# Moving the first two steps of an MoE layer one place earlier between the attention units of a fused kernel

## The chip, the core and the metric

The kernel runs on one core of one Trainium2 chip. The metric is the device time of one launch in microseconds (us), as the median of several executions on the chip. A core has five engines that run their own instruction streams in order and wait for each other by semaphores: TensorE (PE in the profile, with its weight loads as PEld), VectorE (DVE), ScalarE (ACT), GpSimd (POOL) and SyncE (SP), whose queue here issues every DMA.

## What is computed

A sliding-window attention with a few sink positions, whose output is the input of two dense two-matrix layers (called MoE in the code, though there is no routing):

```
scores = q @ k.T / 8                       # 2 batches, 8 heads, 768 positions, head size 64
keep   = key position < n_sink  or  0 <= distance < window      # 4 and 128
a      = softmax(where(keep, scores, -1e9));   x = a @ v        # x: 1536 tokens x 512
h = x @ w1_in;   x = (h * tanh(softplus(h))) @ w1_out           # 512 -> 2048 -> 512
h = x @ w2_in;   out = (h * clip(h + 3, 0, 6) / 6) @ w2_out
```

The weights come as 64-bit floats in HBM and are decoded on the core.

## The kernel before

**Tiling.** The 1536 tokens are twelve units of 128 positions of one batch. They are grouped into three blocks of four units, `BLOCKS = [[6, 7, 0, 1], [2, 3, 4, 5], [8, 9, 10, 11]]`; the MoE layers work on a block (512 tokens) at a time. All values that go into an MoE matmul are split into two fp16 halves, and each product is three matmuls (high by high, high by low, low by high).

**The first eight units** (blocks 0 and 1) are computed by the class `First` in fp32 and are emitted by `first_blocks` in the order 6, 7, 0, 1, 2, 3, 4, 5; its loop variable `n` counts them from 0, so n = 5, 6, 7 are units 3, 4 and 5. For each unit it emits `turn(0)` (transposes of the exponentials of heads 0 to 3, line 315, copied out of PSUM by ACT at 317 and DVE at 319; the sink columns at 323 to 326), the next unit's `scores(0)` (line 296; row minimum on DVE 300, exponential on ACT 304), the `outputs` of the unit before (line 356 transposes the result, 359 and 360 write it into the block's `xt`), `values(0)` (334 and 341), `turn(1)`, the next unit's `scores(1)`, `values(1)`, and `normalise` (347 to 350). The last unit, n = 7, has no next unit, so no scores lie between its parts.

**The last four units** (block 2) are emitted in small pieces by `gen_front` and `gen_back` in fp16, between the halves of later MoE steps, from the moment `open_late` has opened their buffers. Those buffers take the memory of the first units, so their first load (`load_unit`, 411) waits for the last `normalise`. Keys and queries of a late unit are loaded (411), split on ACT and DVE (431/432 for k, 439/440 for v, 457/458 for q), and transposed by a DMA (434 for `kt`, 460 for `qt`); the sinks go through `gen_sinks` (520 to 542, four small loads `vsn` among them). Then come the scores (480), minimum (487), exponential (494), the transposed probabilities `atg` (511) and the values (557 to 568).

**An MoE step** (`moe_steps`) takes two chunks of 128 of the 2048 inner columns for one block. `up` is 24 matmuls of 512 columns into two PSUM tiles (666 to 668), then the activation: for the first layer ACT 670 on each half, 678, 679, 680, DVE 683 twice, ACT 689 (high half of `g16`), DVE 690 (low half). `down` is 24 matmuls (725) that read that `g16`; it is emitted one step later (`LAG = 1`). Before a step, the weights it needs are decoded (208 to 210 and 216 on DVE, 213 on ACT), from two raw buffers that SP fills (166 and 170, 512 KB each). `hook`, called amid the steps, emits further pieces of weight decoding and, once the late buffers are open, of the late units.

**Order.** The generator `moe` is advanced by `next(moe)` inside `first_blocks` for its first two steps and run to its end after it. `up` of these steps reads block 0, which is complete with the `outputs` of n = 3, emitted at n = 4. What is written here is only the order of emission: the tile framework schedules the instructions and sets the order in which they stand on each engine.

Of the kernel before, what the change touches and what calls it, by code (L numbers as in the profile page):

```python
# [29 lines left out]
def attention_moe_moe2(  # L30
# [30 lines left out]
    w_a = main.enter_context(tc.tile_pool(name="w_a", bufs=KF // 2))  # L61
    st_p = main.enter_context(tc.tile_pool(name="st", bufs=STB))
    dec_p = main.enter_context(tc.tile_pool(name="dec", bufs=1))
    part_p = main.enter_context(tc.tile_pool(name="part", bufs=NPART))
    e_p = main.enter_context(tc.tile_pool(name="e", bufs=2))
    g_p = main.enter_context(tc.tile_pool(name="g", bufs=LAG + 1))
    ps_acc = main.enter_context(tc.tile_pool(name="ps_acc", bufs=4, space=PSUM))
# [95 lines left out]
    def fetch_w(layer, f):  # L163
        wi, wo = wsrc[layer]
        t = st_p.tile([128, 2, 512, 2], I32, tag="raw", name="raw")
        nc.sync.dma_start(
            out=t[:, 0].rearrange("p (k f) t -> p k (f t)", k=KD),
            in_=wi[:, f * 256:(f + 1) * 256].rearrange("(k p) f -> p k f", p=128),
        )
        nc.sync.dma_start(out=t[:, 1].rearrange("p f t -> p (f t)"), in_=wo[f * 128:(f + 1) * 128, :])  # L170
        return t

    def load_w():
        if nload[0] >= len(wseq):
            return
        layer, f = wseq[nload[0]]
        nload[0] += 1
        raw_t[layer, f] = fetch_w(layer, f)
# [9 lines left out]
    def gen_check():  # L188

        ahead = []  # L190
        for f in range(KF):
            ahead.append((f, fetch_w(0, f)))
            if len(ahead) > STB - 1:
                g, t = ahead.pop(0)
# [40 lines left out]
    def load_first(u, names="kqv"):  # L235
        b, i = divmod(u, NSB)
        rows = slice(i * 128, (i + 1) * 128)
        for nm, src, pool, tag in (("k", k, n_p, "n"), ("q", q, n_p, "n"), ("v", v, v_p, "v")):
            if nm in names:
                t = pool.tile([128, H, D], F32, tag=tag, name="first")  # L240
                nc.sync.dma_start(out=t, in_=src[b, :, rows, :].rearrange("h p d -> p h d"))
                qkv_n.setdefault(u, {})[nm] = t
# [121 lines left out]
    def first_blocks():  # L364
        us = [First(u) for u in first]
        for u in us[:2]:
            u.prep()
        us[0].scores(0)
        us[0].scores(1)
        for n, e in enumerate(us):  # L370
            f = us[n + 1] if n + 1 < len(us) else None
            if n + 4 < len(us):
                load_first(first[n + 4])
            e.turn(0)
            if f:
                f.scores(0)
            if f is None:
                next(moe)
            if n > 0:
                us[n - 1].outputs()  # L380
            e.values(0)
            if n + 2 < len(us):
                us[n + 2].prep()
            e.turn(1)
            if f:
                f.scores(1)
            if n == len(us) - 2:
                next(moe)
            e.values(1)
            e.normalise()  # L390
        us[-1].outputs()
# [303 lines left out]
    def down(st, span):  # L695
        layer, blk, f = st
        T = len(blocks[blk]) * 128
        per = per_bank(blk)
        g2 = gt.pop(st)
        fa, fb = span  # L700
        if f == fa:
            acc[layer, blk] = [ps_acc.tile([128, per * T if layer == 0 else DM], F32, tag="acc", name="acc") for _ in range(KD // per if layer == 0 else T // 128)]
        a = acc[layer, blk]

        parts = [(n, m) for n in range(len(a)) for m in range(per if layer == 0 else 1)]
        for i in range(2 * per):
            g16 = g2[:, :, i]
            w = wt[layer, 1, f + i]
            first, last = f + i == fa, f + i == fb - 1
            for c, (n, m) in enumerate(parts):  # L710
                if layer == 0:
                    wh = w[:, 0, c * 128:(c + 1) * 128]
                    wl = w[:, 1, c * 128:(c + 1) * 128]
                    mm = [(wh, g16[:, 0]), (wh, g16[:, 1]), (wl, g16[:, 0])]
                    o = a[n][:, m * T:(m + 1) * T]
                    end = m == per - 1
                else:
                    gh = g16[:, 0, c * 128:(c + 1) * 128]
                    gl = g16[:, 1, c * 128:(c + 1) * 128]
                    mm = [(gh, w[:, 0]), (gh, w[:, 1]), (gl, w[:, 0])]  # L720
                    o = a[n]
                    end = True
                for x, (l_, r_) in enumerate(mm):

                    nc.tensor.matmul(o, l_, r_, start=first and m == 0 and x == 0, stop=last and end and x == 2, skip_group_check=True)  # L725
                if last and end:
                    finish(layer, blk, n, a[n], span)
            if i % per == per - 1:
                hook()
# [39 lines left out]
    load_first(first[3])  # L769
    for _ in range(STB - 1):  # L770
        load_w()
# [24 lines left out]
    def moe_steps():  # L796
        pend = []
        fmax = 0
        for s, (cur, span) in enumerate(steps):
            layer, j, f = cur  # L800
            fend = layer * KF + f + 2 * per_bank(j)
            fmax = max(fmax, fend)
            stage = [x[:4] for x in STAGES].index((layer, j) + span)
            budget["lim"] = 2 * (fmax + AHEAD[stage])
            budget["chk"] = stage >= CHECK and not raw_t
            if f == span[0] and layer == 0 and j >= 2:
                att_side.until(("unit", blocks[j][-1]))
            budget["att"] = RATES[stage]
            dec_side.until(("dec", fend - 1))
            up(cur)  # L810
            yield
            pend.append((cur, span))
            while len(pend) > LAG:
                down(*pend.pop(0))
        for st in pend:
            down(*st)

    moe = moe_steps()
    first_blocks()
    p1.close()  # L820
    open_late()
# [179 lines left out]
STAGES = [(0, 0, 0, 4), (0, 1, 0, 10), (0, 0, 4, 16), (0, 1, 10, 16), (0, 2, 0, 16), (1, 0, 0, 8), (1, 1, 0, 8), (1, 0, 8, 16), (1, 1, 8, 16), (1, 2, 0, 16)]  # L1001
CHECK = 8
LAG = 1
STB = 2
P1N = 8
NWARM = 12
# [40 lines left out]
```

## Time and profile before

| | |
|---|---|
| Median of three runs | 624.52 us (624.19 to 625.42) |
| The profiled execution's own time | 623.05 us |
| Its span, first to last instruction | 621.3 us |
| PE busy in the span | 600.8 us, 97% |
| DVE, ACT, POOL busy | 376.0, 354.6, 14.2 us |
| Granted TensorE clock, mean | 0.998 of full speed |

The span lies 1.75 us below the execution's own time, and the profiled execution 1.47 us below the median of the runs. Times in the rows below count from the start of the span. Busy time is the time that an engine spends in instructions that the profile counts; ends of matmuls are modelled. The first eight attention units run until about 98.8 us, the first layer's steps on blocks 0 and 1 and the late units lie behind that, and the second layer fills the rest.

### The profile page before, as it was taken

How to read it: one execution, taken by the hardware profiler on the slowest of the kernel's cores; microseconds unless marked ns; L12 is line 12 of the kernel's file. 1: busy time of each engine (PE TensorE's matmuls, PEld its weight loads, DVE VectorE, ACT ScalarE, POOL GpSimd, SP SyncE). 2: the span in 40 equal slices, each digit the busy share in tenths (PEclk: the TensorE clock that was granted, in tenths of full speed). 3: DMA queues.
4: the chain of work that ended last, by engine and by line, in shares of the span. 5: the costliest groups of instructions: out<-in, count | busy, mean ns of one | idle time of the engine just before them, and what ended most of it. 6: DMA issues, size and time to landing. Idle time of an engine off the chain costs nothing.

```text
span 621.3 us, 8731 instructions
## 1 busy us (share of the span) xinstructions
PE 600.8 (97%) x3400; PEld 307.6 (50%) x3400; DVE 376.0 (61%) x688; ACT 354.6 (57%) x640; POOL 14.2 (2%) x28
## 2 busy tenths in 40 slices
PE   8999999899989999899999999999999999999995
PEld 5888865444444445444444444444444444444442
DVE  5678787889988554626988999844432322422221
ACT  5887676887788676647686765453343331413131
POOL 0010000600000000000000000000000000000000
PEclk9999999999999999999999999999999999999999
DMA  9865146897479313100344434598800100100002
GB/s 188 195 130 170 69 143 150 218 244 210 135 205 205 55 37 54 37 18 0 136 136 136 148 124 152 193 333 304 304 0 1 44 25 0 69 1 0 1 0 73
DMA packets 105832, 72.10 MB, mean 116 GB/s; under 512 B 73512, under 2 KB 98088, under 8 KB 105784
## 3 DMA queue, kind: packets, MB, share of 16 engines
q1 hardware_dynamic: 105784, 71.48, 41.3%
q8 instruction: 28, 0.46, 0.3%
q14 instruction: 20, 0.16, 0.1%
HBM read 60.43 MB, written 3.15 MB: 102 GB/s over the span
## 4 chain that ended last, share of the span: by engine, by line
PE 68%; DVE 14%; ACT 9%; DMA 4%; issue 3%; SPq 1%; ACTq 0%; DVEq 0%
PE acc L725 27%; PE h L666 9%; PE h L668 9%; PE h L667 9%; PE o L341 4%; PE s L296 3%; DVE g L690 2%; DVE e L683 2%; PE tp L315 2%; DVE p L209 2%; DVE p L210 2%; ACT w L213 1%; ACT e L678 1%; ACT e L679 1%; DVE w L216 1%
## 5 line engine op out<-in xcount | busy, mean ns | idle before, releaser
L666 PE MATMUL h<-xt,w 128*128 128x512 f16 x384 | 145.6, 379 | 1.3 <-DVE e L683 1.3
L667 PE MATMUL h<-xt,w 128*128 128x512 f16 x384 | 145.5, 379 | 0.0
L668 PE MATMUL h<-xt,w 128*128 128x512 f16 x384 | 145.5, 379 | 0.0
L725 PE MATMUL acc<-g,w 128*128 128x512 f16 x576 | 129.5, 379 | 2.7 <-DVE g L690 2.2
L725 PE MATMUL acc<-w,g 128*128 128x512 f16 x576 | 128.1, 379 | 0.0
L685 DVE SCALAR_TENSOR_TENSOR e<-e,h 128x512 f32<-128x512 f32 x48 | 32.8, 686 | 97.8 <-ACT e L672 97.8
L725 PEld LDWEIGHTS <-g 128*128 128x128 f16 x576 | 56.3, 98 | 68.0
L725 PEld LDWEIGHTS <-w 128*128 128x128 f16 x576 | 55.4, 98 | 69.0 <-issue 3.8
L672 ACT ACTIVATE e<-h,bias 128x512 f32<-128x512 f32 x48 | 32.7, 683 | 95.7 <-PE h L668 95.7
L690 DVE SCALAR_TENSOR_TENSOR g<-e,g 128x1024 f16<-128x1024 f32 x48 | 58.7, 1223 | 25.1 <-ACT g L689 24.9
L689 ACT ACTIVATE g<-e 128x1024 f16<-128x1024 f32 x48 | 50.6, 1055 | 31.7 <-DVE e L685 17.9
L668 PEld LDWEIGHTS <-w 128*128 128x128 f16 x384 | 37.6, 98 | 45.2
L667 PEld LDWEIGHTS <-w 128*128 128x128 f16 x384 | 37.6, 98 | 44.7 <-issue 1.3
L666 PEld LDWEIGHTS <-w 128*128 128x128 f16 x384 | 37.6, 98 | 44.6
L216 DVE SCALAR_TENSOR_TENSOR w<-p,w 128x1024 f16<-128x1024 f32 x32 | 39.1, 1222 | 14.5 <-ACT w L213 14.5
L213 ACT ACTIVATE w<-p 128x1024 f16<-128x1024 f32 x32 | 33.7, 1053 | 21.5 <-DVE p L210 21.1
L670 ACT ACTIVATE e<-h 128x512 f32<-128x512 f32 x48 | 28.3, 589 | 25.6 <-PE h L668 25.3
L186 ACT ACTIVATE y<-y 128x512 int32<-128x512 int32 x32 | 20.0, 625 | 37.0 <-DVE y L184 36.9
L683 DVE SCALAR_TENSOR_TENSOR e<-e,h 128x512 f32<-128x512 f32 x48 | 30.7, 681 | 16.9 <-ACT e L680 16.9
L209 DVE SCALAR_TENSOR_TENSOR p<-raw,p 128x1024 int32<-128x1024 int32 x32 | 39.1, 1223 | 0.7
L210 DVE SCALAR_TENSOR_TENSOR p<-raw,p 128x1024 int32<-128x1024 int32 x32 | 39.1, 1222 | 0.3
L304 ACT ACTIVATE d<-d,mins 128x272 f32<-128x272 f32 (+2 forms) x64 | 30.4, 479 | 6.6 <-DVE mins L300 6.6
(141 smaller groups left out, 582.6 us busy)
## 6 DMA issues: line engine op xcount, KB each, us to landing
raw<-in_moe_w_in_dram SPq DMA_DIRECT2D x48, 512.0 KB, 3.9
raw<-in_moe_w_out_dram SPq DMA_DIRECT2D x48, 512.0 KB, 5.1
first<-in_k_dram SPq DMA_DIRECT2D x8, 256.0 KB, 5.2
first<-in_q_dram SPq DMA_DIRECT2D x8, 256.0 KB, 5.0
first<-in_v_dram SPq DMA_DIRECT2D x8, 256.0 KB, 5.2
out_dram<-part SPq DMA_DIRECT2D x8, 256.0 KB, 2.2
nk<-in_k_dram SPq DMA_DIRECT2D x5, 256.0 KB, 3.2
nv<-in_v_dram SPq DMA_DIRECT2D x5, 256.0 KB, 4.2
```

What stands on the lines that cost most here:

```text
L209: nc.vector.scalar_tensor_tensor(out=p, in0=lo_w, scalar=29, in1=p, op0=ALU.logical_shift_right, op1=ALU.bitwise_or)
L210: nc.vector.scalar_tensor_tensor(out=p, in0=hi_w, scalar=-0x40000000, in1=p, op0=ALU.bitwise_and, op1=ALU.bitwise_or)
L213: nc.scalar.activation(out=w[:, :, 0, :], in_=pf, func=AF.Copy, scale=2.0 ** SW)
L216: nc.vector.scalar_tensor_tensor(out=w[:, :, 1, :], in0=pf, scalar=2.0 ** SW, in1=w[:, :, 0, :], op0=ALU.mult, op1=ALU.subtract)
L666: nc.tensor.matmul(o, wh, x[:, 0, c, :], start=c == 0, stop=False)
L667: nc.tensor.matmul(o, wh, x[:, 1, c, :], start=False, stop=False)
L668: nc.tensor.matmul(o, wl, x[:, 0, c, :], start=False, stop=c == KD - 1)
L683: nc.vector.scalar_tensor_tensor(out=e[:, i], in0=e[:, i], scalar=2.5, in1=hps[i], op0=ALU.subtract, op1=ALU.mult)
L685: nc.vector.scalar_tensor_tensor(out=e[:, i], in0=e[:, i], scalar=6.0, in1=hps[i], op0=ALU.min, op1=ALU.mult)
L689: nc.scalar.activation(out=gh, in_=e, func=AF.Copy, scale=sc)
L690: nc.vector.scalar_tensor_tensor(out=gl, in0=e, scalar=sc, in1=gh, op0=ALU.mult, op1=ALU.subtract)
L725: nc.tensor.matmul(o, l_, r_, start=first and m == 0 and x == 0, stop=last and end and x == 2, skip_group_check=True)
```

## The change

`first_blocks` advances `moe` for the units in the new constant `FILL = (5, 6)`, each time between `turn(1)` with the next unit's `scores(1)` and `values(1)`. The first step moves from n = 6 to n = 5 (unit 4 to unit 3). The second moves from n = 7 (unit 5), where it stood behind `turn(0)`, to n = 6 (unit 4). Nothing else is edited; the same instructions are in both programs. Lines behind the removed ones have numbers smaller by two in the changed kernel (668 for 670, 723 for 725).

```diff
             e.turn(0)
             if f:
                 f.scores(0)
-            if f is None:
-                next(moe)
             if n > 0:
                 us[n - 1].outputs()
...
             e.turn(1)
             if f:
                 f.scores(1)
-            if n == len(us) - 2:
+            if n in FILL:
                 next(moe)
             e.values(1)
             e.normalise()
...
+FILL = (5, 6)
```

The scheduled order changes on every engine from the first moved step to about 250 us; behind that it is the same but for buffer and semaphore choices. Three places matter to what follows.

On PE, the end of the first eight units, before (`d`, `ds` are exponentials, `tp` transposes in PSUM, `ats` sink columns, `xf` a unit's normalised result):

```order
L356 MATMUL tp<-ident,xf 128x128 x4
L334 MATMUL o<-vsb_331,ats 128x256
L341 MATMUL o<-first,at 128x64 x8
L315 MATMUL tp<-ident,d 128x128 x8
L325 MATMUL tp<-ident,ds 64x128
L334 MATMUL o<-vsb_331,ats 128x256
L341 MATMUL o<-first,at 128x64 x8
L356 MATMUL tp<-ident,xf 128x128 x4
```

and in the changed kernel, from the values of unit 4 on:

```order
L341 MATMUL o<-first,at 128x64 x8
L315 MATMUL tp<-ident,d 128x128
L325 MATMUL tp<-ident,ds 64x128
L356 MATMUL tp<-ident,xf 128x128 x4
L315 MATMUL tp<-ident,d 128x128 x4
L334 MATMUL o<-vsb_331,ats 128x256
L341 MATMUL o<-first,at 128x64 x8
L315 MATMUL tp<-ident,d 128x128 x4
L325 MATMUL tp<-ident,ds 64x128
L334 MATMUL o<-vsb_331,ats 128x256
L341 MATMUL o<-first,at 128x64 x8
L356 MATMUL tp<-ident,xf 128x128 x4
```

Before, the second step's 24 matmuls stood right ahead of the first row; now they stand ahead of the values of unit 4, and nothing but two short transposes parts those values from the transposes (356) that need them.

On SP, the queue behind the first loads of the late units (numbers tell the tiles apart: kt1_1439 and qt_1489 are what the first late scores read), before:

```order
L520 DMA ksn_1331<-in_k_dram 16x8x64
L411 DMA nq_1430<-in_q_dram 128x8x64
L434 DMA_TRANSPOSE kt1_1397<-k16_1394 128x8x128
L411 DMA nk_1432<-in_k_dram 128x8x64
L525 DMA_TRANSPOSE ks_1_1336<-k16s_1333 128x8x16
L530 DMA vsn_1359<-in_v_dram 64x1x64 x4
L166 DMA raw_1406<-in_moe_w_in_dram 128x4x256
L170 DMA raw_1406<-in_moe_w_out_dram 128x1024
L411 DMA nv_1434<-in_v_dram 128x8x64
L434 DMA_TRANSPOSE kt1_1439<-k16_1436 128x8x128
L460 DMA_TRANSPOSE qt_1489<-q16_1486 128x8x128
```

and in the changed kernel:

```order
L518 DMA ksn_1331<-in_k_dram 16x8x64
L166 DMA raw_1406<-in_moe_w_in_dram 128x4x256
L432 DMA_TRANSPOSE kt1_1397<-k16_1394 128x8x128
L170 DMA raw_1406<-in_moe_w_out_dram 128x1024
L523 DMA_TRANSPOSE ks_1_1336<-k16s_1333 128x8x16
L528 DMA vsn_1359<-in_v_dram 64x1x64 x4
L409 DMA nq_1430<-in_q_dram 128x8x64
L409 DMA nk_1432<-in_k_dram 128x8x64
L409 DMA nv_1434<-in_v_dram 128x8x64
L458 DMA_TRANSPOSE qt_1489<-q16_1486 128x8x128
L409 DMA nq_1493<-in_q_dram 128x8x64
L432 DMA_TRANSPOSE kt1_1439<-k16_1436 128x8x128
```

The pair of weight loads has gone ahead, into the places of the first `nq` and the second `nk`, and these two now stand behind the sinks' transpose and the four `vsn` loads.

On ACT and PE, the third MoE step (`g_1448` is its activation) around those first late scores, before. ACT:

```order
L678 ACTIVATE e<-e,one 128x1024
L536 ACTIVATE vsh<-vsn 128x128
L679 ACTIVATE e<-e,fifth 128x1024
L680 ACTIVATE e<-e 128x1024
L737 ACTIVATE part<-acc 128x512 x3
L213 ACTIVATE w<-p 128x2x512
L689 ACTIVATE g_1448<-e 128x1024
```

ACT in the changed kernel:

```order
L676 ACTIVATE e<-e,one 128x1024
L534 ACTIVATE vsh<-vsn 128x128
L677 ACTIVATE e<-e,fifth 128x1024
L455 ACTIVATE q_1486<-nq 128x512
L678 ACTIVATE e<-e 128x1024
L735 ACTIVATE part<-acc 128x512
L429 ACTIVATE k_1436<-nk 128x512
L735 ACTIVATE part<-acc 128x512 x2
L687 ACTIVATE g_1448<-e 128x1024
```

PE in the changed kernel, just ahead of the first late scores:

```order
L666 LDWEIGHTS w
L666 MATMUL h<-xt_89,w 128x512
L723 LDWEIGHTS w
L723 MATMUL acc<-g_1448,w 128x512
L723 LDWEIGHTS w
L723 MATMUL acc<-g_1448,w 128x512
```

The splits of the first `nq` and the second `nk` now stand inside the third step's activation, and seven of the matmuls (723) that read that activation stand on PE ahead of the first late scores, where before there was none.

## Rows read from the trace of the kernel before

**Rows 1.** The page, parts 1 and 2: engines' busy time; granted clock by slice.
```profile
PE 600.8 (97%) x3400; PEld 307.6 (50%) x3400; DVE 376.0 (61%) x688; ACT 354.6 (57%) x640; POOL 14.2 (2%) x28
...
PEclk9999999999999999999999999999999999999999
```

**Rows 2.** Waits of PE: total us, times, longest.
```profile
PE acc L725 <- DVE g L690: 2.2, 2, 1.4
PE s L480 <- DMA qt<-q: 1.8, 1, 1.8
...
PE h L666 <- DVE e L683: 1.3, 1, 1.3
```

**Rows 3.** Timeline of PE, unit 5: start, us, instruction, count, [idle before, releaser].
```profile
94.90 0.70 PE L334 MATMUL o<-vsb,ats 64*128 64x256 f32 x2 [0.38 <-DVE ats L326]
...
96.19 1.77 PE L341 MATMUL o<-first,at 128*128 128x64 f32 x14 [0.23 <-ACT at L317]
98.75 0.66 PE L356 MATMUL tp<-ident,xf 128*128 128x128 f32 x4 [0.79 <-DVE xf L350]
```

**Rows 4.** Timeline of SP's queue from the first late load on.
```profile
98.78 0.37 SPq L411 DMA_DIRECT2D nk<-in_k_dram  x1
...
100.80 0.43 SPq L411 DMA_DIRECT2D nq<-in_q_dram  x1
...
106.74 1.14 SPq L525 DMA_TRANSPOSE ks<-k16s  x1
107.97 2.33 SPq L530 DMA_DIRECT2D vsn<-in_v_dram  x4
110.42 0.39 SPq L166 DMA_DIRECT2D raw<-in_moe_w_in_dram  x1
...
115.97 1.29 SPq L460 DMA_TRANSPOSE qt<-q  x1
```

**Rows 5.** Chain of waits by time, late loads until they land: start, us, what.
```profile
98.78 3.23 DMA nk<-in_k_dram
...
109.78 2.20 DMA vsn<-in_v_dram
...
117.31 3.48 DMA nq<-in_q_dram
```

**Rows 6.** Timeline of ACT, the third step's activation and a later split of q.
```profile
112.08 0.31 ACT L536 ACTIVATE vsh<-vsn 128x128 f16<-128x128 f32 x1 [0.50 <-DMA vsn<-in_v_dram]
...
113.47 1.06 ACT L680 ACTIVATE e<-e 128x1024 f32<-128x1024 f32 x1
114.43 1.56 ACT L737 ACTIVATE part<-acc 128x512 f32<-128x512 f32 x3
...
116.81 1.07 ACT L689 ACTIVATE g<-e 128x1024 f16<-128x1024 f32 x1
...
120.88 0.63 ACT L457 ACTIVATE q<-nq 128x512 f16<-128x512 f32 x1 [1.50 <-DMA nq<-in_q_dram]
```

**Rows 7.** Timeline of DVE, the same step.
```profile
114.56 1.28 DVE L683 SCALAR_TENSOR_TENSOR e<-e,h 128x512 f32<-128x512 f32 x2 [0.28 <-ACT e L680]
...
118.11 1.22 DVE L690 SCALAR_TENSOR_TENSOR g<-e,g 128x1024 f16<-128x1024 f32 x1
```

**Rows 8.** Line 434, the key transposes: ns min/median/max, and DMA to landing.
```profile
L434 SPq DMA_TRANSPOSE kt<-k x5: 1237/1632/3629, 103.7 to 187.4; - x5
...
DMA to landing us min/median/max: 3.3/4.9/5.8
```

**Rows 9.** Timeline of PE: start-up, first late scores, a later step.
```profile
1.26 5.30 PE L777 MATMUL wp<-warm 128*128 128x512 f16 x12 [1.26 <-DVE ones L837]
...
99.25 5.34 PE L725 MATMUL acc<-g,w 128*128 128x512 f16 x24
...
119.34 0.53 PE L480 MATMUL s<-kt,qt 64*128 64x128 f16 x12 [1.80 <-DMA qt<-q]
...
140.45 0.38 PE L666 MATMUL h<-xt,w 128*128 128x512 f16 x1 [1.31 <-DVE e L683]
```

## The prediction, made before the changed kernel had run

> **What bounds the kernel now.** I read the page first: PE is busy 600.8 of 621.3 us at full granted clock in every slice [rows 1], so all the idle time of PE is about 20 us and every microsecond that the change brings or takes must be PE idle time; both programs hold the same matmuls. Second, the waits of PE [rows 2]: the ones near the moved steps are the wait of the first late scores for `qt` (1.8), one of an `up` for the activation's `e` (1.3), and two of a `down` for the low half `g` (2.2 together). Third, PE's timeline [rows 3]: in unit 5, the last of the first eight, PE sits out 0.38, 0.23 and 0.79 us, in all 1.40. Fourth, SP's queue [rows 4] and the chain of waits [rows 5], which show what the 1.8 us hang on. When the last `normalise` has ended, the first late load goes out at 98.78; I call this moment T0, and count from it in both kernels. Then a chain of loads, splits and transposes runs until the first late scores at 119.34, which stood ready from 119.34 − 1.80 = 117.54 [rows 9], that is T0 + 18.76. So two stretches decide: up to T0, where PE's order is short of cover, and from T0 to the first late scores, where SP's queue is in order.
>
> **The change, part by part.** *Matmuls, activations and decoding of the moved steps.* Each `up` is 24 matmuls of about 0.22 us (5.34 for 24 [rows 9]), before and after; what was 5.3 us of cover at one place is 5.3 us at another. Weights that are decoded earlier cost DVE and ACT nothing net: with 61% and 57% busy [rows 1] both have room, and what they delay is priced in the terms below. The pair of raw loads that goes ahead on SP takes 0.39 and 0.50 us of its queue [rows 4]; its price lies in what then stands behind, term B.
>
> *Term A, the end of the first eight units.* Before, the second step's matmuls separated the values of unit 4 from the transposes (356) of the same unit, and lay ahead of the last unit. In the changed order only two short transposes do. A unit's result waits 0.79 for `xf` when nothing covers it [rows 3]; the two transposes take about 0.3, so I put +0.45 on unit 4. The `ats` copy of unit 4 now has the first step's low half ahead of it on DVE, 1.22 us [rows 7]; a similar copy without that in its way made PE wait 0.38 [rows 3]. I take half of 1.22, +0.6, since the first step's matmuls run while part of it is done; the ends are 0 and 1.22. In unit 5 the 0.38 and 0.79 stay; the 0.23 (behind ACT's copies) goes, as ACT has the second step's activation behind it earlier: −0.23. Sum +0.8. The lower end is −0.6 (0.23 and 0.38 both gone, nothing new), the upper +2.0 (0.79, all of 1.22).
>
> *Term B, the first late scores.* This is the largest. Before, the first `nq` went out at 100.80, T0 + 2.0, and `vsn` at 107.97 [rows 4]. In the changed queue `nq` and the second `nk` stand behind the sinks' transpose and `vsn`. That transpose waits for DVE; it issued at 106.74, T0 + 7.96 [rows 4], and as the order ahead of it on ACT and DVE is nearly that of before, I take T0 + 8.4 (8.0 to 9.2). The first `vsn` followed 1.23 later and the next queue entry 2.45 behind that (110.42 − 107.97), so `nq` goes out at T0 + 12.1 in place of T0 + 2.0. A later `nq` took 3.48 to land [rows 5]: T0 + 15.6. Its split on ACT is 0.63 [rows 6]: 16.2. And now ACT, in order, has the third step's activation behind that split: 1.06 for 680 [rows 6] to 17.2, 1.28 for the pair 683 on DVE [rows 7] to 18.5, while ACT does three copies of 1.56 together and the split of the second `nk` (0.63 as for q; neighbours overlap by 0.1), to about 19.0; then 689, 1.07 [rows 6], to 20.1, and 690 on DVE, 1.22 [rows 7], to 21.35. Seven `down` matmuls that read `g` now stand ahead of the scores: the first needs the high half, the second the low half, the other six end some 1.3 later, T0 + 22.7. The keys: `nk` at T0 + 12.5, landed with the 3.23 of the first one [rows 5] at 15.8, split on ACT behind 680 and a copy at 18.15, on DVE behind the pair 683 at some 19.2; SP has sent `qt` (1.29 [rows 4]) and another `nq` by then. So `kt` goes out at T0 + 19.2, and the five key transposes landed 3.3, 4.9 (median) or 5.8 us from issue [rows 8]: T0 + 22.5, 24.1 or 25.0. Without idle time PE would be through the seven matmuls (7 × 0.22 = 1.5) at T0 + 18.8 + 1.5 = 20.3. The scores start at the later of 22.7 and the landing: idle 2.4, 3.8 or 4.7, against 1.80. I take the median, since the queue is as full here as at the other four transposes: B = +2.0, from +0.6 to +2.9.
>
> The Trainium skill bears on this in "Advanced Engine Details and Errata", section "X-Bar Transpose (TRN2)": a transposing DMA is said to be as fast as a regular one. By the trace it is not: the quickest of five keys' transposes (3.3 us) equals the loads of `nk` (3.2), and the median is 4.9 [rows 5, 8]. By the page B would be its lower end, +0.6.
>
> *Term C.* Before, an `up` matmul waited 1.31 us at 140.45 for `e` of its own activation's buffer [rows 9]. PE comes there later by terms A and B, while DVE and ACT go on: the wait shrinks by what PE lost. −1.3, from −1.3 to 0.
>
> *Term D, new waits behind.* Later steps' `down` and later late scores stand in another order until some 250 us, and late loads come 2 us or more later to them. Nearest rows: two waits of a `down` for `g`, 2.2 in all, longest 1.4 [rows 2]. I take half of the longest, +0.7, from 0 to 1.4.
>
> *Sum:* 0.8 + 2.0 − 1.3 + 0.7 = +2.2 us on the profiled execution of 623.05, 625.25. The median of the runs lies 1.47 above that execution, so the time is 624.52 + 2.2 = **626.7**. All lower ends together give −0.6 + 0.6 − 1.3 + 0 = −1.3 (623.2), all upper ends 2.0 + 2.9 + 0 + 1.4 = +6.3 (630.8).
>
> **The rivals.** (1) *Worse:* the order behind the late scores suffers too; the 1.31 of term C is not repaid as ACT and DVE are late as well, and D takes its upper end. With A +0.8, B at its upper end 2.9, and D 1.4 that is +5.1, 629.6. For it speaks that ACT stands still in order while it waits for `nq`: the later split of a q cost it 1.50 idle [rows 6]. Against: ACT and DVE have two fifths of their time to catch up [rows 1].
>
> (2) *No change:* the key transpose lands at its minimum, 3.3 us from issue, and the seven matmuls end last: B +0.6, sum +0.8, 625.3. It is decided by whether `kt` is through by T0 + 22.7. For it: one of five did it in 3.3; against: the median of 4.9 [rows 8]. By the Trainium skill's section named above this would be the rule; so far the rows are against it.
>
> (3) *Faster:* the MoE work leaves ACT and DVE before the late units arrive, and the late chain finds both engines free, so that `nq` and the second `nk` are split as soon as they land and both transposes are down before PE has come to T0 + 20.3. Then the 1.80 and the 1.31 vanish, and with A at 0 and D at 0 the sum is −3.1, 621.4. It decides at an issue of `kt` before T0 + 20.3 − 3.3 = 17.0, so of `nk` at about T0 + 10 or earlier. For it: before, the chain of waits ran for 8 us through splits by ACT and DVE that queued behind MoE work. Against: SP's queue holds `nk` behind `vsn` in either engine's best case; with the sinks' transpose at T0 + 8.0, `nk` is at 12.1.
>
> (4) *The clock:* PE sat out 1.80 us with the granted clock at full level [rows 1, 9]; the idle I forecast is split by the first of the seven matmuls, its largest part under 2.5. If it fell nevertheless, 24 matmuls at the half level, 0.44 us each as in the warm-up (5.30 for 12 [rows 9]), would cost +5.3 beside the sum: 632.0. The Trainium skill, "TensorE: Matmul & The Clock Gate", section "HAM oscillation — how this bites in real kernels", warns that waits on DMA let the clock fall; no row of this trace shows it.
>
> That the change does nothing is excluded by the changed rows of the order on PE and SP.
>
> **How the numbers follow.** Forecast +2.2 (626.7): 0.58. Worse (629.6): 0.15. No change (625.3): 0.17. Faster (621.4): 0.08. Clock (632.0): 0.02. A measurement of this kernel can tell 0.2%, 1.25 us, from no change. The forecast and the two worse cases lie beyond that, 0.75; no change is 0.17; faster 0.08. The range leaves out the faster case, the clock and half of the worse one, 0.18: from 624.4, below the no-change case and about where the forecast's terms B and D are both at their lower ends with A at 0.8 (+0.1), to 629.4, where B and D are at their upper ends and half of the 1.31 is not repaid (+0.8 + 2.9 + 1.4 − 0.65 = +4.5, 629.0, with 0.4 for the spread of runs).
>
> **What would show it.** In the changed profile, PE's timeline should show a wait of about half a microsecond of 356 for `xf` of unit 4 and one for `ats` ahead of 334. On SP's queue the first `nq` should come behind `vsn`, 12 us after the first late load and not 2. PE should wait for `g` at the seven `down` matmuls and then for `kt`, not `qt`, at the first late scores, 3.8 us in all. The 1.31 at 140 should be gone. The prediction is wrong if the scheduled `nq` lands early or ACT isn't held by it, if `kt` lands before the `down` matmuls have ended, or if the idle time at the late scores is no larger than 1.80.

## The result, and the profile of the changed kernel

The changed kernel takes 627.98 us (median of 20 runs, 625.57 to 630.37) against 624.48 us for the kernel before on the same chip (20 runs). The ratio is 1.0051, with a 95% interval of 1.0039 to 1.0063: 2.4 to 3.9 us slower. The forecast was slower, 626.7 in a range of 624.4 to 629.4, so time and direction hold. The medians lie 3.5 us apart, where the forecast had 2.2. The profiled execution took 628.35 us, with a span of 626.6 us against 621.3. Of these 5.3 us, 4.7 lie ahead of TensorE's last matmul, and they are what the following takes apart. From the start of that matmul to the end of the span the traces of all runs take 6.4 to 7.4 us with the same instructions; why this varies is open.

The page of the changed kernel, parts 1 and 2 (compare [rows 1]):

```profile
PE 604.0 (96%) x3400; PEld 307.7 (49%) x3400; DVE 377.0 (60%) x688; ACT 354.5 (57%) x640; POOL 15.3 (2%) x28
...
PEclk9999998999998999999999999999999999999998
```

PE is busy 3.2 us longer with the same 3400 matmuls, and two slices amid the run, from 94 and from 188 us on, have a clock below full level. Neither was in the sum of the forecast, which took every microsecond to be idle time of PE; the clock stood among the rivals, at a chance of 0.02. The waits of PE in the changed kernel (total us, times, longest):

```profile
PE acc L723 <- DVE g L688: 3.9, 4, 1.4
PE s L478 <- DVE mins L485: 1.7, 1, 1.7
...
PE tp L356 <- DVE xf L350: 1.4, 2, 0.8
...
PE acc L723 <- ACT g L687: 1.1, 3, 0.5
...
PE o L334 <- DVE ats L326: 0.5, 1, 0.5
...
PE o L334 <- DVE e L681: 0.4, 1, 0.4
PE s L478 <- DMA kt<-k: 0.3, 1, 0.3
```

Against [rows 2], the wait for `qt` and the one of an `up` for `e` are gone, the waits for `g` have grown, and the one for the row minima has gathered in one place. Before, that one was

```profile
PE s L480 <- DVE mins L487: 1.6, 2, 1.4
```

and in PE's timeline

```profile
185.42 0.21 PE L480 MATMUL s<-kt,qt 64*128 64x128 f16 x1 [1.45 <-DVE mins L487]
185.79 0.51 PE L480 MATMUL s<-kt,qt 64*128 64x128 f16 x11 [0.15 <-DVE mins L487]
```

SP's queue of the changed kernel (compare [rows 4]):

```profile
100.58 0.37 SPq L409 DMA_DIRECT2D nk<-in_k_dram  x1
...
110.32 2.33 SPq L528 DMA_DIRECT2D vsn<-in_v_dram  x4
112.70 0.46 SPq L409 DMA_DIRECT2D nq<-in_q_dram  x1
113.20 0.58 SPq L409 DMA_DIRECT2D nk<-in_k_dram  x1
...
119.51 1.43 SPq L432 DMA_TRANSPOSE kt<-k  x1
```

T0, the first late load, lies at 100.58 in place of 98.78. `nq` goes out 12.12 us behind it, where the forecast had 12.1, and the key transpose 18.9 behind it (forecast 19.2).

PE's two stretches at the lower clock level (stretch, its length, busy us and count of PE, then of PEld, DVE, ACT and POOL, granted clock, DMA share, GB/s):

```profile
100.00:102.00 2.00, 1.45 (x6) 1.11 (x7) 1.97 (x3) 0.30 (x1) 0.00 (x0) 0.54 0.10 23
102.00:104.00 2.00, 2.00 (x7) 0.69 (x6) 1.49 (x2) 1.36 (x2) 0.00 (x0) 0.60 1.13 241
...
186.00:188.00 2.00, 0.38 (x2) 0.09 (x1) 1.97 (x5) 1.28 (x2) 0.00 (x0) 1.00 0.82 326
188.00:190.00 2.00, 1.73 (x15) 0.84 (x15) 2.00 (x6) 1.89 (x5) 0.00 (x0) 0.73 0.03 8
190.00:192.00 2.00, 2.00 (x6) 0.71 (x5) 2.00 (x6) 2.00 (x6) 0.00 (x0) 0.50 0.57 140
```

From 190 to 192 us, all at 0.50 (1.2 GHz in place of 2.4), only 6 matmuls are under way. The first fall comes with the wait for the last `xf`, the second behind a wait of 1.75 us for the row minima of a late unit.

### The profile page after: what moved, and what is told of

It is laid out like the page before. It is cut to its first block, busy times and chain, and to the rows that moved or that the text cites. A ratio compares the mean times of both kernels' runs of the same rounds, so it can differ in the third digit from the quotient of the medians.

```text
span 626.6 us, 8727 instructions
## 1 busy us (share of the span) xinstructions
PE 604.0 (96%) x3400; PEld 307.7 (49%) x3400; DVE 377.0 (60%) x688; ACT 354.5 (57%) x640; POOL 15.3 (2%) x28
## 4 chain that ended last, share of the span: by engine, by line
PE 66%; DVE 13%; ACT 7%; issue 7%; DMA 4%; POOL 1%; SPq 1%; DVEq 0%; ACTq 0%
PE acc L723 27%; PE h L664 9%; PE h L666 9%; PE h L665 9%; PE o L341 4%; PE s L296 3%; DVE p L209 2%; PE tp L315 2%; DVE g L688 2%; DVE e L681 1%; DVE p L210 1%; ACT w L213 1%; DVE w L216 1%; DVE p L208 1%; ACT e L676 1%
## 5 line engine op out<-in xcount | busy, mean ns | idle before, releaser
L723 PE MATMUL acc<-g,w 128*128 128x512 f16 x576 | 132.6, 385 | 5.1 <-DVE g L688 3.9
L184 DVE TENSOR_SCALAR y<-raw 128x1024 int16<-128x1024 int16 x32 | 22.2, 692 | 19.9 <-DMA raw<-in_moe_w_out_dram 18.7
```

## The experiments

Two theories stood at the start. ORDER: the loss is idle time of TensorE that the new order makes, as forecast. CLOCK: much of it comes from falls of the granted clock that the change causes. Each kernel ran beside the kernel before on the same chip. "Clock" is the mean granted clock of one execution. By the traces it is 0.997 or 0.998 when the clock does not fall behind the start-up, 0.994 or 0.995 with one fall, and 0.992 or less with two or one long one. Executions with 0.996 or more are called "without a fall"; no trace has a mean of 0.996 or 0.993, so there the line is a choice.

**1. The kernel before, once more.** No edit.

> The kernel before, once more, for the span and granted clock of each of its runs. Theory ORDER (the loss of the change is idle time of TensorE that the new order makes: at the end of the first eight units and at the first late scores): the clock of single runs varies here as it does in the changed kernel, and the changed kernel is some 3.4 us behind at any clock. Theory CLOCK (much of the loss is that the changed kernel makes the granted clock fall to half after the last of the first units, in more than half of its runs): here nearly all runs stand at 0.996 or more with spans of 621.5 to 623.5, and the changed kernel's runs at 0.996 or more (626.0 median) are only some 1.5 us behind.

Measured: 623.40 us (12 runs), ratio 0.9988 (0.9973 to 1.0004). Eight of the 12 runs are below 0.996, and 19 of the 29 runs of the reference beside them: the clock falls in the kernel before too, so that part of CLOCK is refuted, and the change does not fall more often (12 of 20 runs). What differs is the price. Here runs without a fall have a median of 623.25 and the others 624.28; in the changed kernel 626.04 (8 runs) and 628.38 (12 runs). Between these two groups of runs the change is thus 2.8 us behind without a fall and 4.1 with one: neither ORDER's 3.4 at any clock nor CLOCK's 1.5. The trace of this execution has a fall, at the end of the first units:

```profile
98.00:100.00 2.00, 1.28 (x6) 0.82 (x7) 1.86 (x3) 0.47 (x1) 0.00 (x0) 0.78 0.03 7
100.00:102.00 2.00, 2.00 (x6) 0.76 (x5) 1.84 (x3) 1.08 (x2) 0.00 (x0) 0.50 1.12 245
```

and PE's timeline at the first late scores:

```profile
118.81 0.38 PE L668 MATMUL h<-xt,w 128*128 128x512 f16 x1
119.25 0.53 PE L480 MATMUL s<-kt,qt 64*128 64x128 f16 x12
```

The scores start at 119.25, as in [rows 9] (119.34), and with no wait: the 1.65 us that PE lost at the lower level came out of its 1.80 us wait for `qt`. In this trace the fall costs next to nothing, since a wait for something else lies behind it.

**2 and 3. Both steps in one unit.** The change with

```diff
-            if n in FILL:
+            for _ in range(FILL.count(n)):
                 next(moe)
...
-FILL = (5, 6)
+FILL = (6, 6)
```

and with `(5, 5)` for the other kernel.

> Only the second step is moved: both steps stand in n = 6 (unit 4). SP's queue behind the first late load is then that of the changed kernel (nq and the second nk behind vsn), and on TensorE the stretch without 512-column matmuls ahead of the first late load is that of the kernel before, about 9 us in place of 12. Theory ORDER: the late scores lose as in the change, end of the units a little less: 626 to 627.5. Theory CLOCK: no fall of the clock ahead of 110 us, nearly all runs at 0.996 or more there; time 625.5 to 626.5, as the changed kernel's runs without a fall.

> Both steps are moved to n = 5 (unit 3), so the stretch without 512-column matmuls ahead of the first late load grows to about 22 us; SP's queue is that of the changed kernel. Theory ORDER: idle time of TensorE at the end of the units as in the changed kernel or 1 us more, the late scores the same: 627.5 to 629. Theory CLOCK: the clock falls in nearly every run, more than once or for longer in that stretch, mean clock 0.985 or less, 629 to 632.

Measured: both in unit 4 626.69 us, ratio 1.0038 (1.0020 to 1.0055), all 12 runs below 0.996; both in unit 3 626.64 us, ratio 1.0033 (1.0018 to 1.0048), 6 of 12 runs without a fall. That is against CLOCK as stated: the longest stretch without MoE matmuls does not bring the most falls. ORDER has the time of the first right, but not of the second, which is 0.9 us below its range. The end of the first units goes nearly the way ORDER has it. With both steps in unit 4 the last transposes start at 98.45, 0.3 earlier than before; with both in unit 3 at 100.17. Yet both kernels are as slow, so the end of the units is not the whole loss.

**4. The first `nq` and second `nk` sent early.** The change with

```diff
-            load_unit(u - 1, "kv")
+            load_unit(u - 1, "k", "0")
+            load_unit(u, "qk")
+            load_unit(u - 1, "v")
...
             yield from gen_keys(u - 1)
-            load_unit(u)
+            load_unit(u, "v")
```

(the third argument gives the first `nk` a buffer of its own).

> The changed kernel with the first nq and the second nk issued right behind the first nk (a buffer of its own for the first nk). That undoes SP's order alone: TensorE's order up to the first late load is that of the changed kernel. Theory ORDER: the late scores' wait and the seven down matmuls' waits for g go, 1 to 2 us faster than the changed kernel: 626 to 627. Theory CLOCK: the fall after the last unit stays, as often, and its 1.7 us, which the late scores' wait had partly hidden, show in full: no more than 0.5 us faster than the changed kernel in runs with a fall, 1 to 2 us faster in runs without.

Measured: 629.83 us (6 runs, all below 0.996), ratio 1.0077 (1.0047 to 1.0107). That is against both theories. It is not shown to be slower than the change (1.0051, 1.0039 to 1.0063), as the intervals overlap, but the gain that ORDER forecast did not come. SP's queue of this kernel shows the first reason:

```profile
100.53 0.37 SPq L409 DMA_DIRECT2D nk<-in_k_dram  x1
100.94 0.58 SPq L409 DMA_DIRECT2D nq<-in_q_dram  x1
101.56 0.71 SPq L409 DMA_DIRECT2D nk<-in_k_dram  x1
...
114.06 1.14 SPq L525 DMA_TRANSPOSE ks<-k16s  x1
115.32 2.31 SPq L530 DMA_DIRECT2D vsn<-in_v_dram  x4
118.17 1.29 SPq L434 DMA_TRANSPOSE kt<-k  x1
119.51 1.31 SPq L460 DMA_TRANSPOSE qt<-q  x1
```

The two loads now go out by T0 + 1, but in exchange ACT's split of the sinks stands behind the third step's exponential, the sinks' transpose goes out at T0 + 13.5 in place of 8.5, and `kt` and `qt` stand behind it, at T0 + 17.6 and T0 + 19.0. PE waits 2.00 for `qt`. A larger wait comes later in this trace, and the clock falls to half with it (0.50 from 146 to 148 us):

```profile
145.48 0.58 PE L666 MATMUL h<-xt,w 128*128 128x512 f16 x1 [2.71 <-DVE e L683]
```

The late chain has more than one strand; freeing one puts another at its end. As the edit moved other waits too, this run does not show what SP's order alone costs.

**5. A longer wait in the kernel before.**

```diff
                     c += w_
+                if u == last[1] and h0 == 4: nc.vector.tensor_copy(out=d[:, 0, 0:n], in_=sps[0])
```

> The kernel before, with one copy of 128x272 on VectorE put ahead of the row minima of one late unit's third pair of heads, so that the wait of the scores for these minima at about 185 us grows from 1.45 to about 1.9 us, what it is in the changed kernel. The copy's result is overwritten. Theory WAIT ALONE: 0.4 to 0.5 us slower than the kernel before, 623.8 to 624.5, falls of the clock no more frequent. Theory FALL (the longer wait there is followed by a fall of the granted clock in more of the runs, and a fall there costs 2.0 us in full since no wait behind it gives it back): a mean clock below 0.996 in most runs, median 625 to 626.5, with runs that differ by about 2 us.

Measured: 626.58 us (12 runs), ratio 1.0027 (1.0012 to 1.0042). One run is without a fall (624.02); ten have a clock of 0.992 or less, against 10 of 30 of the reference. FALL holds in the number of falls, and its range for the median is passed by 0.08 us. The trace of this kernel, PE's timeline and the stretches behind:

```profile
186.34 0.87 PE L479 MATMUL s<-kt,qt 64*128 64x128 f16 x12 [1.79 <-DVE mins L487]
```

```profile
186.00:188.00 2.00, 1.52 (x16) 0.87 (x16) 2.00 (x6) 1.68 (x4) 0.00 (x0) 0.95 0.04 10
188.00:190.00 2.00, 2.00 (x6) 0.68 (x5) 2.00 (x6) 2.00 (x6) 0.00 (x0) 0.50 0.45 115
```

The wait is 0.35 us longer than in run 1 (1.44), and the median 2.5 us higher than the reference's (624.07). Ahead of the wait PE lies 0.58 us behind the kernel before in this trace, behind the fall 2.59. Of these 2.0 us, 0.34 are the longer wait and 1.68 the fall, and they are never given back. An earlier fall of this trace, at 100 us, cost 1.68 as well and was given back at the first late scores; the 0.58 came at 141.02, where an `up` waits 1.89 for `e` (1.31 before), and why it does is not shown.

**6. The first step alone moved**, the second at its old place.

```diff
-            if n == len(us) - 2:
+            if n == 5:
                 next(moe)
```

> Only the first step is moved, to n = 5 (unit 3); the second stays at n = 7 (unit 5), where its 24 matmuls stand between the values of unit 4 and the transposes of its result. Theory GAP (the idle time at the end of the first units comes from the second step's leaving this place): the first late load goes out at 98.5 to 99.0 as before, what is left is the late part; 624 to 625.5. Theory PLACE OF THE FIRST (the first step's activation and weight decoding, a unit earlier, delay VectorE and ScalarE there): the first late load at 99.8 or later and a time as the changed kernel's, 626 to 628.

Measured: 627.98 us (7 runs), ratio 1.0063 (1.0040 to 1.0087). GAP falls, and the time lies where PLACE OF THE FIRST has it, but not for its reason: although the second step's matmuls cover unit 4 as before, the last transposes start at 100.02. The waits in PE's timeline there (unit 5) add up to 0.38 + 0.78 = 1.16, less than the 1.40 of [rows 3]. The time is in busy PE. The stretch from 63.9 us to the last transposes in this kernel

```profile
63.90:100.02 36.12, 34.76 (x238) 24.67 (x236) 27.67 (x63) 26.56 (x52) 0.00 (x0) 1.00 0.32 112
```

and in the kernel before:

```profile
63.90:98.75 34.85, 33.39 (x238) 24.23 (x236) 26.02 (x61) 25.48 (x51) 0.00 (x0) 1.00 0.35 119
```

The same 238 matmuls take 1.37 us more. By line, the scores (296) are busy 5.62 us against 5.07, the transposes of the exponentials (315) 5.55 against 5.04, the values (341) 10.48 against 10.31. Timelines of PE in one unit show an example, in this kernel

```profile
75.52 0.74 PE L296 MATMUL s<-kt,qt 64*128 64x128 f32 x8
76.19 0.66 PE L356 MATMUL tp<-ident,xf 128*128 128x128 f32 x4
76.69 0.27 PE L315 MATMUL tp<-ident,d 128*128 128x128 f32 x1
76.89 1.02 PE L296 MATMUL s<-kt,qt 64*128 64x128 f32 x8
```

and before:

```profile
69.65 1.21 PE L296 MATMUL s<-kt,qt 64*128 64x128 f32 x16
70.79 0.66 PE L356 MATMUL tp<-ident,xf 128*128 128x128 f32 x4
```

Sixteen score matmuls, which use 64 of the 128 rows each, took 1.21 us in one run of instructions and 0.74 + 1.02 in two groups. The single starts in the traces show two things behind this. In the sixteen, and in the first eight of this kernel, the matmuls start in pairs 7 ns apart; in the second eight no two start together. And from a transpose to a score matmul it takes 0.20 us from start to start (76.69 to 76.89), where transposes follow each other at 0.11, so each further change of kind costs about 0.1. Why the pairs are torn apart is not shown. Over the whole stretch the extra time goes with the place of the first step: with it in unit 3 the 238 matmuls are busy 34.76 us here, 34.58 in run 3 and 34.25 in run 8; with it in unit 4, 33.08 in run 2, 33.29 in run 7 and 33.39 in the kernel before.

**7. The second step later**, ahead of the last `values(1)`: the change with `FILL = (6, 7)`.

> The first step as before (n = 6), the second moved the other way: behind turn(1) of the last unit, ahead of its values(1). Its matmuls then cover the waits for ats and at of unit 5, and the transposes of unit 4 lose their cover in part. Theory GAP: the first late load within 0.6 us of 98.8; late scores with fourteen down matmuls ahead, so a late part 0.5 to 1 us slower: 623.5 to 625.5. Theory SP QUEUE (what counts is whether nq and nk stand behind vsn, as here and in the changed kernel): 626 to 627.

Measured: 626.60 us (12 runs), ratio 1.0031 (1.0014 to 1.0049); without a fall 625.23. The last transposes start at 98.69, as GAP has it, but by 180 us TensorE is 0.83 us late, the wait for the minima there is 1.92, and in this trace the clock falls behind it. The time lies in SP QUEUE's range and above GAP's, but not for SP QUEUE's reason: at the first late scores PE waits no longer than before (0.61 and 0.45 us for `g`, none for the transposes).

**8. The changed kernel, once more.**

> The changed kernel once more, for a second trace of it. Where this execution's clock doesn't fall at about 189 us, TensorE's shift against the kernel before should be 1.8 us at the first late load, about 2.3 behind the first late scores, and 2.4 to 2.8 at the end; where it falls there, 2 us more from there on.

Measured: 626.79 us (10 runs), ratio 1.0043 (1.0025 to 1.0061). This execution is without a fall, and gives the sum of the order alone: a shift of 1.76 us at the last transposes, 2.31 behind the first late scores and 2.83 at the end, against 1.8, 2.3 and 2.4 to 2.8 expected. PE's timeline:

```profile
79.23 0.70 PE L334 MATMUL o<-vsb,ats 64*128 64x256 f32 x2 [0.42 <-DVE e L681]
...
92.45 0.66 PE L356 MATMUL tp<-ident,xf 128*128 128x128 f32 x4 [0.64 <-DVE xf L350]
...
97.11 0.70 PE L334 MATMUL o<-vsb,ats 64*128 64x256 f32 x2 [0.45 <-DVE ats L326]
...
100.51 0.66 PE L356 MATMUL tp<-ident,xf 128*128 128x128 f32 x4 [0.78 <-DVE xf L350]
...
120.60 0.81 PE L723 MATMUL acc<-g,w 128*128 128x512 f16 x3 [1.30 <-ACT g L687]
121.88 1.02 PE L723 MATMUL acc<-g,w 128*128 128x512 f16 x4 [0.48 <-DVE g L688]
123.15 0.53 PE L478 MATMUL s<-kt,qt 64*128 64x128 f16 x12 [0.24 <-DMA kt<-k]
...
137.76 4.69 PE L723 MATMUL acc<-g,w 128*128 128x512 f16 x21 [1.32 <-DVE g L688]
...
188.10 0.87 PE L478 MATMUL s<-kt,qt 64*128 64x128 f16 x12 [1.94 <-DVE mins L485]
```

and, once more as a stretch up to the last transposes:

```profile
63.90:100.51 36.61, 34.25 (x238) 24.21 (x236) 30.35 (x66) 26.48 (x52) 0.00 (x0) 1.00 0.32 113
```

PE's last matmul starts at 617.68 here, 2.83 us behind the kernel before (614.85); in the trace with two falls it starts at 619.59, 1.9 us later. The two traces are of one program: the first fall costs 1.5 us, which are given back at the wait of 1.30 at 120.60, and the second 1.7, which stay.

**9 and 10. The minima first.** The changed kernel and the kernel before with

```diff
-        nc.vector.tensor_scalar(out=p, in0=hi_w, ...)
+        with tc.issue_after(late["mn"].pop()) if len(late.get("mn", ())) == 1 else ExitStack():
+            nc.vector.tensor_scalar(out=p, in0=hi_w, ...)
```

where `mn` is the instruction for the minima that the scores wait for, and the weights are the third ones decoded after its emission.

> The changed kernel, with the row minima of that late unit's third pair of heads put ahead of the next weights' first two decoding operations on VectorE (0.69 and 1.22 us), so that the wait of the scores at 188 us, 1.75 to 1.94, goes. TensorE's order stays. Theory FALL: without the wait the clock doesn't fall there in any run; 1.9 us of wait and, in more than half of the runs, 2.0 us of half clock go: median 624.3 to 625.3 and runs closer together. Theory WAIT ALONE (falls come at some other place, as often): the 1.9 us of the wait go, the spread stays, median 625.3 to 626.3.

> The kernel before with the same edit: its wait of 1.45 and 0.15 us at 185 us goes. Theory FALL: 1.5 us of wait and the falls behind it go, median 621.7 to 622.5, the fastest runs 621.5 to 622; runs with a mean clock of 0.993 or less gone. Rival MOVED WAIT (the decoding that is put off makes a later step wait for its weights): 623 to 624.

Measured: the change 627.80 us (6 runs), ratio 1.0055 (1.0037 to 1.0073), one run without a fall; the kernel before 623.81 us (12 runs), ratio 0.9992 (0.9979 to 1.0005). Nothing is gained. MOVED WAIT is right for the kernel before, and for the change both theories are 1.5 us or more too low. PE's timeline in the kernel before with the edit:

```profile
185.22 0.53 PE L483 MATMUL s<-kt,qt 64*128 64x128 f16 x12
...
189.78 0.38 PE L671 MATMUL h<-xt,w 128*128 128x512 f16 x1 [1.34 <-DVE e L688]
```

The wait for the minima is gone, and 4.5 us on PE waits 1.34 for DVE's multiplication by `e`, which now stands behind the decoding that was put off. In the stretch from 184 to 192 us DVE is busy for 7.58 of 8 us, so that of these two whichever goes first, PE waits for the other. In the trace of the change with the edit the same wait is 1.43 us, at 191.13. As the wait had only moved, this pair could not show what happens to the falls without one. No kernel here beats the kernel before.

## Why the prediction came out right, point by point

Direction and range hold, and the size in part by luck. The order's own loss is 2.83 us in PE by the trace without a fall (in medians without a fall 2.5 us, 626.04 against 623.58 for the reference of run 1, which is another group of runs, and 3.0 us, 626.67 against 623.71, in the group of run 8), where the forecast had 2.2. Inside it three terms are off, A by +1.0, B by −1.4 and D by +1.1, and these errors cancel but for 0.6.

- **Term A (forecast +0.8)** measures 100.51 − 98.75 = 1.76. The idle time was right: 0.42 + 0.64 + 0.45 + 0.78 = 2.29 against 1.40, so +0.89. The other 0.86 is PE busy longer with the same 238 matmuls (34.25 against 33.39): the scores 0.44 more, the transposes of the exponentials 0.55 more, the values 0.42 less, in an order that breaks up their groups. The step that failed is the premise that all the time must be idle because the matmuls are the same. Runs 2, 3, 6 and 7 show that this part comes with the first step's move, which the forecast gave no price of its own on PE.
- **Term B (forecast +2.0)** is 0.55: the scores start 3.81 us later, less 1.50 for the seven matmuls moved ahead and 1.76 for A. PE sits out 1.30 + 0.48 + 0.24 = 2.02 us there, not the 3.8 of the forecast. The chain was right to T0 + 20: the first of the seven waits 1.30 (some 1.3 by the forecast's times), `nq` and `kt` go out when forecast. The mis-sized step is the landing of `kt`. The median of 4.9 was taken; issued at T0 + 18.9 and used at T0 + 22.5, it took at most 3.6. So the scores start at T0 + 22.6, where the lower bound had 22.7, though not because the seven matmuls end last: `kt` still ends the wait, by 0.24. So the page of the Trainium skill that was weighed there, "Advanced Engine Details and Errata", section "X-Bar Transpose (TRN2)", was nearer for this transpose than the median of the five rows. The forecast set it aside by the loads of `nk` alone (3.2); the profile of the kernel before has medians of 3.2 to 5.2 us for its loads of 256 KB, so the five transposes at 3.3 to 5.8 were no clear case against it.
- **Term C (forecast −1.3)** holds by itself: no `up` waits at 140 us in either trace of the change. But a wait of the same size now stands just ahead of that place, the first one of term D.
- **Term D (forecast +0.7, up to 1.4)** is above its upper end. A `down` waits 1.32 for `g` at 137.76, so that behind 140 us PE is 2.40 us late, nearly as much as the 2.31 behind the first late scores. Then come two places that the forecast did not price: the wait for the row minima, 1.94 against 1.45 + 0.15, and one of 0.18 for `g` at 323.58. In all D is 2.83 − 2.31 + 1.31 = 1.83.
- **The clock rival (chance 0.02)** was wrong in size both ways. Falls come in most executions of both kernels, so a chance of 0.02 was far too low. A fall costs not 5.3 us but 1.5 to 1.7, as it ends within 4 us, in the traces that have a twin without it and the same order up to there. At the first late scores a wait gives it back, at 189 us nothing does. Of 20 runs of the change 12 had a fall, 2.3 us slower in the median. This fits the two measurements, the first 1.3 us above the forecast and the second one on it (626.79, half of its runs without a fall). That a longer wait at that place goes with more falls is shown in the kernel before (run 5; that they come at that place, in one trace); that the change's own falls come from its longer wait was not shown by taking the wait away, since it only moved.
- **Faster and no change** fell as worked out: `nk` went out at T0 + 12.6, far behind the T0 + 10 that the first would have needed. The rival of no change had B right, but A and D too small. Of the **worse** case its D came, and more, but not its B.

## What to carry to other kernels

A reordering that issues the same matmuls can still make TensorE busy longer, so compare the busy time of the two orders and not their waits alone. A sum that comes out near the measured one can hold large errors of both signs, so check it term by term. When a chain passes through several in-order queues, work out the arrival by the slowest strand, and carry the landing of a single transfer as a range (3.3 to 5.8 us here) rather than as a median. A wait that is followed by another wait hides a loss ahead of it; a wait that nothing follows costs in full, with the fall of the clock that may come behind it.

## What the runs showed of the hardware that was not expected

- The granted clock falls to half in most executions of the same program and not in others, at full load but for waits of 0.8 to 2.7 us. Before a fall TensorE had sat out 0.79 us (end of the first units), 1.75 to 1.92 us (at 186 to 188), 2.21 us (run 6, at 121) or 2.71 us (run 4, at 145). The same waits stood without a fall in other executions: 1.94 us in run 8. The price was 1.5 to 1.7 us a fall in the traces of the change and of runs 1 and 5. In run 10 it fell already behind waits of 0.37 and 0.23 us, stayed low from about 97.5 to 104.4 us, and PE lost 2.9.
- Fp32 score matmuls on 64 rows start in pairs 7 ns apart in some groups and one by one in others: eight took 0.74 us in pairs and 1.02 without (run 6).
- A key transpose issued behind a load and another transpose was used 3.6 us after its issue, near the least of the five of [rows 8]. The five of the changed kernel landed after 3.2 to 5.7 us.
